# Attention and a gMLP block on one core: x of the second batch turned by DMA, with a new order of steps

## The chip, the cores and the metric

The kernel runs on one core of a Trainium2 chip. The metric is the time of one execution in microseconds of the device; lower is better. The kernel before took 160.62 us (median of three runs, 160.41 to 160.88).

## The reference

Two blocks follow one another, on 4 batches of 768 positions. The first is attention with 8 heads of 64, where a query sees the 128 last positions and the first 4 ("sinks"). Its output, x (768 x 512 per batch), goes through a gated block with a residual:

```python
keep = is_sink | in_window
scores = np.where(keep, scale * q @ k.T, -1e9)
x = softmax(scores) @ v                       # per head, heads side by side: 768 x 512
h = gelu_tanh(x @ w_in)                       # 768 x 1024
u, v = h[..., :512], h[..., 512:]
v_n = (v - mean(v)) / sqrt(var(v) + 1e-6) * g_ln
v_s = einsum('ts,bsd->btd', w_sg, v_n) + b_sg[None, :, None]
out = x + (u * v_s) @ w_out
```

## The kernel before

**A list of steps.** The order of all the work is written out by hand in one string, `STEPS` (lines 16 to 64), of 659 words. A loop at the end (lines 593 to 598) calls one function per word. A step's instructions join the queue of the engine they run on, each queue runs in the order of the list, and semaphores order the queues among each other. `QK.1.2.0` is the function `QK` with the numbers 1, 2 and 0. The first number is nearly always the batch. A letter at the end names the engine where there is a choice: A for ScalarE (ACT), D for VectorE (DVE), P for GpSimd (POOL); a mask without a letter runs on DVE.

**Loads.** `LQ`, `LK` and `LV` load q, k and v, `LW` the halves of w_in, `LWS` the halves of w_sg and `LWO` w_out. All but the very first are issued by GpSimd, between its other work. At most eight of GpSimd's loads are under way: the trace shows it at rest before a load until the eighth load before that one has landed. `LG` and `LC` load constants by SyncE.

**Attention.** A batch has four pairs of heads, p = 0 to 3. For batches 0 to 2, `TQ` and `TK` (lines 302 to 314) turn q and k of a pair on TensorE, 12 turns into PSUM, and `EQ` and `EK` copy the result out, on ACT or DVE. For batch 3 (`TURN`, line 72) SyncE issues a DMA that turns it (line 318) and there is no `TQ` or `TK`. `QK` makes the scores of two tiles of positions, `EX` takes the exponential on ACT, and `MK` masks, on DVE in one instruction or on POOL in two. `KS`, `SK` and `SX` do the sink scores: `KS` writes the first four keys of all pairs of a batch into a small tile (DVE, four instructions from batch 1 on), `SK` multiplies it by all q of the batch, so it follows the last of the batch's copies of k, and `SX` is its exponential. `AV` multiplies by v, half a batch's positions (three tiles of 128) per step, and `NR` divides and writes x for that pair and half.

**x turned.** The gated block needs x with its columns on the partitions, in the tile `xT`, of which there is one. For batches 0 and 1, `XT` (line 431) turns six blocks of 128 x 128 on TensorE and `XE` (line 438) copies them out of PSUM, on ACT or DVE: four of each per batch. For batches 2 and 3, `XD` (line 442) has SyncE issue one DMA that turns half a batch: three tiles of 512 columns, 12 blocks, 384 KB. It waits for the four `NR` of its half.

**The gated block.** `MV` makes two tiles of the v half of h (eight products, line 453), `GV` its GELU, `BN`, `RS` (POOL) and `NM` the statistics, `Z` the normalised tile, on ACT or DVE. `MV.b.0` needs the first half of x alone, `MV.b.1` both. `MU` and `GU` are the same for u; `MU.b.0` and `MU.b.1` need the first half of x, the others the second. For batch 0 the first `MV` and `MU` are cut in two, with `MA` and `UA`. `SP` multiplies z by w_sg, which `WT` has turned on TensorE and `WE` copied; it needs all of z. `GT` and `GM` do the gate, `OU` the last product, `RA` (DVE) adds x, and `ST` stores a tile of 128 x 512 by SyncE. For batch 3 the last three tiles (`LAST`, line 75) are done in halves, `OU` and `OB`, `RA` and `RB`, `ST` and `SB`.

**Buffers.** PSUM has a ring `mm` of four (lines 134 to 135) for `TQ`, `TK`, `AV`, `XT`, `WT`, `SK`, `SP` and `OU`, and a ring `sc` of two for `QK`, `MV` and `MU`. A step takes the next buffer and waits until its last reader is done. Output tiles `ot` have three buffers, so `RA` waits for the third store before it.

**SyncE's queue** runs the `EQ` and `EK` of batch 3, the `XD` and all stores, in the order of the list.

Of the kernel before, what the change touches and what calls it, by code (L numbers as in the profile page):

```python
# [13 lines left out]


STEPS = """
ZERO IDEN LQ.0.0 LK.0.0 LQ.0.1 FILL LK.0.1 LC VSK MASK LK.0.2 MASK0 CQ.0.0.A LK.0.3 HM.7 TQ.0.0 CK.0.0.A LV.0.0
EQ.0.0.D HM.1 TK.0.0 LQ.0.2 EK.0.0.A TQ.0.1 LQ.0.3 EQ.0.1.D QK.0.0.2 QK.0.0.1 LV.0.1 EX.0.0.2 VSM.0 TK.0.1 LV.0.2
KS.0.0 SK.0.0 TK.0.2 LV.0.3 EK.0.1.A MK.0.0.2.D QK.0.0.0 TK.0.3 EX.0.0.1 EK.0.2.D LQ.1.0 KS.0.1 EX.0.0.0 LW.0 KS.0.2
QK.0.1.1 MK.0.0.1.D SK.0.1 EX.0.1.1 MK.0.0.0 QK.0.1.2 LW.1 TQ.0.2 SX.0.1 QK.0.1.0 EQ.0.2.D MK.0.1.1.P EX.0.1.2  # L20
AV.0.0.0 AV.0.0.1 EK.0.3.A LWS.0 NR.0.0.0 QK.0.2.1 EX.0.1.0 NR.0.0.1 TQ.0.3 MK.0.1.2.P SK.0.2 EQ.0.3.D EX.0.2.1
QK.0.2.0 LQ.1.2 AV.0.1.1 KS.0.3 EX.0.2.0 MK.0.1.0 LWS.1 QK.0.3.1 SK.0.3 NR.0.1.1 EX.0.3.1 AV.0.1.0 MK.0.2.1.P QK.0.3.0
NR.0.1.0 XT.0.2 SX.0.3 QK.0.2.2 EX.0.3.0 XE.0.2.D MK.0.3.1.P XT.0.0 XE.0.0.D TQ.1.0 EX.0.2.2 LK.1.0 QK.0.3.2 MK.0.2.0
TQ.1.1 EQ.1.0.A LK.1.2 MK.0.3.0 AV.0.2.0 EX.0.3.2 LQ.2.0 AV.0.3.0 NR.0.2.0 EQ.1.1.A MK.0.2.2.P MA.0.0 NR.0.3.0 LWO
MK.0.3.2.D XT.0.1 AV.0.2.1 XE.0.1.A AV.0.3.1 NR.0.2.1 MV.0.0 LV.1.0 VSM.3 UA.0.0 GV.0.0 NR.0.3.1 MU.0.0 VSM.1 XT.0.3
VSM.2 WT.0 LG LV.1.1 XE.0.3.A WT.2 BN.0.0 WT.1 GU.0.0 MV.0.2 WE.1 LV.1.2 WE.2 MV.0.1 WE.0 GV.0.2 BN.0.2 MU.0.2 GV.0.1
TQ.1.2 BN.0.1 RS.0.2 GU.0.2 WT.4 MU.0.1 EQ.1.2.A LV.1.3 WE.4 RS.0.1 TQ.1.3 NM.0.2 GU.0.1 TK.1.0 TK.1.1 EQ.1.3.A
Z.0.4.D LV.2.0 WT.5 NM.0.1 Z.0.5.D MU.0.3 EK.1.1.A Z.0.2.D EK.1.0.A Z.0.0.D LV.2.1 TK.1.3 Z.0.3.D GU.0.3 QK.1.0.2 WE.5
TK.1.2 EK.1.3.A Z.0.1.D QK.1.0.1 EK.1.2.D WT.3 EX.1.0.2 LK.2.0 SP.0.0.3 WE.3 KS.1.0 SP.0.0.0 GT.0.0.3 EX.1.0.1
MK.1.0.2.P SP.0.1.1 GT.0.0.0 GM.0.0.3.D LQ.2.2 QK.1.1.2 GM.0.0.0.D QK.1.0.0 TQ.2.1 EX.1.1.2 GT.0.1.1 MK.1.0.1.P TQ.2.0  # L30
EQ.2.1.A SP.0.1.0 GM.0.1.1.D LV.2.2 EX.1.0.0 MK.1.1.2.D QK.1.2.2 GT.0.1.0 SK.1.0 LV.2.3 EQ.2.0.A QK.1.1.1 MK.1.0.0
SP.0.0.2 SX.1.0 GM.0.1.0.P EX.1.2.2 AV.1.0.1 LK.2.2 GT.0.0.2 EX.1.1.1 QK.1.2.1 MK.1.2.2.D AV.1.0.0 LV.3.0 EX.1.2.1
NR.1.0.1 SP.0.1.2 NR.1.0.0 MK.1.1.1.P QK.1.3.2 QK.1.2.0 GT.0.1.2 EX.1.3.2 SP.0.1.3 LV.3.1 MK.1.2.1.D EX.1.2.0
MK.1.3.2.D AV.1.1.1 LV.3.2 GT.0.1.3 AV.1.2.1 MK.1.2.0 QK.1.3.1 QK.1.3.0 LV.3.3 EX.1.3.1 TK.2.1 NR.1.1.1 AV.1.2.0
NR.1.2.1 EK.2.1.A XT.1.2 GM.0.1.2.P QK.1.1.0 NR.1.2.0 XE.1.2.A TK.2.0 MK.1.3.1.P TQ.2.3 EX.1.1.0 EK.2.0.D TQ.2.2
SP.0.0.1 GM.0.1.3.P EQ.2.3.A LQ.3.0 GM.0.0.2.D OU.0.4 EQ.2.2.A MK.1.1.0 EX.1.3.0 GT.0.0.1 OU.0.5 RA.0.4 AV.1.1.0
GM.0.0.1.P RA.0.5 QK.2.0.2 ST.0.4 QK.2.1.2 AV.1.3.1 EX.2.0.2 NR.1.1.0 ST.0.5 LK.3.0 TK.2.3 EX.2.1.2 MK.1.3.0 TK.2.2
# [596 lines left out]
```

## Time and profile before

| what | value |
|---|---|
| median of three runs | 160.62 us |
| the profiled execution, in all | 160.88 us |
| its span, first to last instruction | 159.2 us |
| granted TensorE clock | 0.995 of full speed |
| turns of x on TensorE (line 436), both batches | 48, 4.1 us busy |
| copies of turned x out of PSUM, ACT / DVE | 5 of 806 ns / 3 of 555 ns |
| copies of turned q and k, ACT / DVE | 17 of 811 ns / 7 of 954 ns |
| masks, DVE (line 382) / POOL (lines 386 and 390) | 26 of 745 ns / 22 pairs, the first of each 668 ns |
| `XD`, DMA from issue to landing, least / median / most | 3.6 / 3.7 / 5.3 us |
| stores, the same | 1.8 / 2.3 / 6.6 us |

The profile tells, of one execution on the chip, when each instruction ran and, from semaphores, what released an engine that stood idle. An engine's busy time is a sum over its instructions. Where the text speaks of a step's time, it is found by counting an engine's instructions off against the list.

The order of time: batch 0's attention until 28 us, batch 0's gated block beside batch 1's attention until about 70, batch 1's `MV` and `MU` from 69.5 to 81.8, batch 2's from 99 to 113 and batch 3's from 128 to 140. The last loads land at 84.5. Batch 0's `XT` steps run from 19.7 to 28.4, batch 1's from 56.2 to 68.4.

### The profile page before, as it was taken

To read this page: it belongs to the slowest core of one execution; us is meant where nothing else is said; L and a number is where in the kernel's file an instruction comes from. 1 tells how busy PE (TensorE), PEld (TensorE's weight loads), DVE (VectorE), ACT (ScalarE), POOL (GpSimd) and SP (SyncE) were. 2 spreads that over 40 slices of the span, in tenths; PEclk is the share of its full clock that TensorE was granted. 3 is DMA by queue.
4 is the path that set the end of the run, shared out by engine and by line. 5 is a ranking of instruction groups with operands and counts; after the bars stand their busy time and mean duration, and the time that the engine had idled before them with its cause. 6 is when DMAs were issued, how large, how long until landed. Compare 5 with 4: busy or idle time off the path is not lost.

```text
span 159.2 us, 3831 instructions
## 1 busy us (share of the span) xinstructions
PE 146.4 (92%) x1516; PEld 86.8 (55%) x1528; DVE 127.9 (80%) x302; ACT 102.9 (65%) x121; POOL 86.6 (54%) x119
## 2 busy tenths in 40 slices
PE   4947899899999899999999999999999999999980
PEld 1435566556656566545565664445656654555640
DVE  5467998979998999965997996389989946988661
ACT  3579997478988498896887658945984225580000
POOL 7998995349398999992303675004057310302620
PEclk9999999999999999999999999999999999999997
DMA  4999999999999999999999548310300590120145
GB/s 159 181 149 164 189 210 204 208 245 204 175 144 166 181 175 155 222 191 217 152 119 176 115 84 199 116 66 13 123 0 1 102 296 1 66 97 37 53 151 198
DMA packets 63442, 22.70 MB, mean 143 GB/s; under 512 B 51392, under 2 KB 60608, under 8 KB 63424
## 3 DMA queue, kind: packets, MB, share of 16 engines
q0 software_dynamic: 45488, 11.80, 83.5%
q1 hardware_dynamic: 17936, 10.66, 28.1%
q8 instruction: 12, 0.20, 0.5%
q14 instruction: 6, 0.05, 0.1%
HBM read 24.81 MB, written 6.29 MB: 195 GB/s over the span
## 4 chain that ended last, share of the span: by engine, by line
PE 69%; DMA 14%; DVE 7%; POOL 5%; issue 3%; DVEq 0%; SPq 0%
PE mm L538 19%; PE sc L505 12%; PE sc L453 12%; PE mm L554 9%; DMA wsg_gated<-in_moe_w_sg_dram 8%; PE sc L367 5%; DMA v_sb<-in_v_dram 5%; PE mm L308 3%; PE mm L407 3%; DVE ot L562 2%; PE mm L413 2%; PE mm L528 2%; PE mm L417 2%; POOL k L195 1%; DMA out_dram<-ot 1%
## 5 line engine op out<-in xcount | busy, mean ns | idle before, releaser
L375 ACT ACTIVATE P<-sc 128x1024 bf16<-128x1024 f32 (+1 forms) x48 | 43.9, 963 | 12.4 <-PE sc L367 12.3
L538 PE MATMUL mm<-wsgT,z 128*128 128x384 bf16 x192 | 34.2, 326 | 0.0
L386 POOL TENSOR_SCALAR_AFFINE_SELECT P<-P 128x512 bf16<-128x512 bf16 x22 | 14.7, 668 | 20.2 <-ACT P L375 14.6
L538 PEld LDWEIGHTS <-z 128*128 128x128 bf16 x192 | 17.8, 98 | 12.1 <-issue 1.4
L554 PE MATMUL mm<-w_out_sb,wsg_gated 128*128 128x512 bf16 (+1 forms) x102 | 23.0, 354 | 1.3 <-POOL wsg_gated L548 0.7
L543 DVE SCALAR_TENSOR_TENSOR gtmp<-mm,g_sb,b_bc 128x384 bf16<-128x384 f32 x32 | 19.5, 613 | 5.0 <-PE mm L538 4.8
L505 PE MATMUL sc<-xT,w_in_sb 128*128 128x384 bf16 x128 | 22.9, 326 | 0.0
L476 DVE BATCH_NORM_STATS2 st<-vt 128x6 f32<-128x512 f32 x24 | 16.2, 676 | 7.4 <-ACT vt L467 7.4
L453 PE MATMUL sc<-w_in_sb,xT 128*128 128x512 bf16 x92 | 21.8, 379 | 0.2
L484 POOL TENSOR_TENSOR rs<-rs,neg_half 128x2 f32<-128x2 f32 (+1 forms) x8 | 6.9, 867 | 27.1 <-DVE rs L479 26.2
L562 DVE TENSOR_TENSOR ot<-mm,x_sb 128x512 f32<-128x512 f32 (+1 forms) x27 | 16.6, 628 | 5.4 <-PE mm L554 5.1
L548 POOL TENSOR_TENSOR wsg_gated<-gtmp,uT 128x384 bf16<-128x384 bf16 x14 | 13.1, 942 | 11.4 <-DVE gtmp L543 11.3
L221 POOL DMA_DIRECT2D v_sb<-in_v_dram x16 | 16.6, 1046 | 4.9 <-DMA wsg_gated<-in_moe_w_sg_dram 1.7
L382 DVE TENSOR_TENSOR P<-P,mask 128x1024 bf16<-128x1024 bf16 (+1 forms) x26 | 19.1, 745 | 0.0
L427 DVE TENSOR_TENSOR x_sb<-mm,rcp 128x384 bf16<-128x384 f32 x32 | 17.8, 557 | 1.1
L467 ACT ACTIVATE vt<-sc 128x1024 f32<-128x1024 f32 x12 | 12.2, 1023 | 9.9 <-PE sc L453 9.9
L521 ACT ACTIVATE uT<-sc 128x768 bf16<-128x768 f32 x16 | 12.8, 806 | 7.6 <-PE sc L505 7.6
L407 PE MATMUL mm<-v_sb,P 128*128 128x65 bf16 x192 | 16.7, 194 | 0.7 <-DVE x_sb L427 0.3
L505 PEld LDWEIGHTS <-w_in_sb 128*128 128x128 bf16 x128 | 12.4, 98 | 8.8
L407 PEld LDWEIGHTS <-P 128*128 128x128 bf16 x192 | 14.3, 98 | 4.6 <-issue 1.9
L367 PE MATMUL sc<-qT,kT 64*128 64x256 bf16 x192 | 15.5, 264 | 0.8 <-ACT kT L226 0.6
L413 PE MATMUL mm<-v_sb,P 128*128 128x65 bf16 x160 | 15.5, 194 | 0.8 <-POOL P L390 0.8
(77 smaller groups left out, 224.6 us busy)
## 6 DMA issues: line engine op xcount, KB each, us to landing
out_dram<-ot SPq DMA_DIRECT2D x21, 256.0 KB, 3.3
v_sb<-in_v_dram POOLq DMA_DIRECT2D x16, 192.0 KB, 11.6
q<-in_q_dram POOLq DMA_DIRECT2D x4, 384.0 KB, 12.7
k<-in_k_dram POOLq DMA_DIRECT2D x4, 384.0 KB, 14.5
wsg_gated<-in_moe_w_sg_dram POOLq DMA_DIRECT2D x2, 576.0 KB, 14.8
w_in_sb<-in_moe_w_in_dram POOLq DMA_DIRECT2D x2, 512.0 KB, 11.8
qn<-in_q_dram POOLq DMA_DIRECT2D x4, 192.0 KB, 11.2
kn<-in_k_dram POOLq DMA_DIRECT2D x4, 192.0 KB, 9.9
```

The costliest lines, as they stand in the source:

```text
L367: nc.tensor.matmul(sc[:, hl, 256 * jl:256 * jl + n], kT[b, p][rows, 128 * j:128 * (j + 1)], qT[b, p][rows, 128 * j:128 * j + n], start=Tru ...
L375: nc.scalar.activation(out=pt[:, :, 0:w], in_=sc_ring[b, p, g][:, :, 0:w], func=AF.Exp, scale=scale)
L382: nc.vector.tensor_mul(pt[:, :, 0:w], pt[:, :, 0:w], m.unsqueeze(1).to_broadcast([128, 2, w]))
L407: nc.tensor.matmul(av[:, il, hl, :], P[b, p, i // 2][:, hl, 256 * (i % 2):256 * (i % 2) + 128], vb[:, h, i, :], start=first, stop=False)
L413: nc.tensor.matmul(av[:, il, hl, :], P[b, p, j // 2][:, hl, 256 * (j % 2) + 128:256 * (j % 2) + 256], vb[:, h, j, :], start=False, stop=False)
L427: nc.vector.tensor_mul(xs[:, 3 * half:3 * half + 3, :].rearrange("p t (h d) -> p t h d", h=H)[:, :, heads(b, p), :], av[:, :, :, 0:Dh], rc ...
L453: nc.tensor.matmul(hp[:, jl, :], xT[b][:, j, c, :], w_in_sb[:, c, d_half:2 * d_half], start=(c == 0), stop=(c == KD - 1))
L505: nc.tensor.matmul(hp[:, n, 0:NH], w_in_sb[:, c, 128 * dc:128 * (dc + 1)], xT[b][:, 3 * hf:3 * hf + 3, c, :], start=(c == 0), stop=(c == K ...
L538: nc.tensor.matmul(ps[:, 0:NH], z[b][:, si, 128 * dc:128 * (dc + 1)], wsgT[:, si, NH * hf:NH * (hf + 1)], start=(si == 0), stop=(si == NT ...
L543: nc.vector.scalar_tensor_tensor(out=gtmp.new((b, hf, dc)), in0=mm_ring["g", b, hf, dc][:, 0:NH], scalar=g_sb[:, dc:dc + 1], in1=b_bc[:, N ...
L554: nc.tensor.matmul(mm_ring["o", b, t][:, cols], gatedT[:, (2 * b + hf) % 3, dc, 128 * tl:128 * (tl + 1)], w_out_sb[:, dc, cols], start=(dc ...
L562: nc.vector.tensor_add(ot.get((b, t))[:, cols], mm_ring["o", b, t][:, cols], x_sb[b][:, t, cols])
```

## The change

Only the list differs: 653 words after, in a new order from end to end. Every function is as it was.

- **x of batch 1.** `XT.1.0` to `XT.1.3` (24 turns) and their copies `XE.1.0.D`, `XE.1.1.A`, `XE.1.2.A` and `XE.1.3.A` are gone; `XD.1.0` and `XD.1.1` are new. x of batch 0 is still turned on TensorE.
- **Engines.** Copies of turned q and k: 17 on ACT and 7 on DVE before, 13 and 11 after. Copies of batch 0's x: 2 on ACT and 2 on DVE before, 1 and 3 after. `CK` moves from ACT to DVE. Masks: 26 on DVE and 22 on POOL before, 29 and 19 after. `GM`: 18 on DVE and 14 on POOL before, 16 and 16 after. `Z`: 8 on ACT and 16 on DVE before, 9 and 15 after.
- **Order of GpSimd's loads.** Before: LQ.0.1, LK.0.1 to 0.3, LV.0.0, LQ.0.2, LQ.0.3, LV.0.1 to 0.3, LQ.1.0, LW.0, LW.1, LWS.0, LQ.1.2, LWS.1, LK.1.0, LK.1.2, LQ.2.0, LWO, LV.1.0. After: LQ.0.1, LK.0.1 to 0.3, LQ.0.2, LQ.0.3, LV.0.0, LQ.1.0, LV.0.1 to 0.3, LW.0, LW.1, LWS.0, LWS.1, LK.1.0, LK.1.2, LQ.1.2, LQ.2.0, LWO, LV.1.0. For batch 3 LK.3.2 comes last in place of LQ.3.2.
- **SyncE's queue** between batch 0's stores and batch 2's x. Before: ST.0.4, 0.5, 0.3, 0.0, 0.2, EQ.3.1, EQ.3.0, EK.3.0, EK.3.2, ST.0.1, EK.3.3, EQ.3.2, EQ.3.3, EK.3.1, XD.2.0. After: ST.0.0, 0.1, 0.2, XD.1.0, XD.1.1, ST.0.4, 0.3, EQ.3.0 to 3.3, ST.0.5, EK.3.0 to 3.3, XD.2.0.
- **The last three tiles** are done in halves in both lists, with the same steps.

The start and the middle of the list, old and then new:

```diff
-ZERO IDEN LQ.0.0 LK.0.0 LQ.0.1 FILL LK.0.1 LC VSK MASK LK.0.2 MASK0 CQ.0.0.A LK.0.3 HM.7 TQ.0.0 CK.0.0.A LV.0.0
-EQ.0.0.D HM.1 TK.0.0 LQ.0.2 EK.0.0.A TQ.0.1 LQ.0.3 EQ.0.1.D QK.0.0.2 QK.0.0.1 LV.0.1 EX.0.0.2 VSM.0 TK.0.1 LV.0.2
-KS.0.0 SK.0.0 TK.0.2 LV.0.3 EK.0.1.A MK.0.0.2.D QK.0.0.0 TK.0.3 EX.0.0.1 EK.0.2.D LQ.1.0 KS.0.1 EX.0.0.0 LW.0 KS.0.2
-QK.0.1.1 MK.0.0.1.D SK.0.1 EX.0.1.1 MK.0.0.0 QK.0.1.2 LW.1 TQ.0.2 SX.0.1 QK.0.1.0 EQ.0.2.D MK.0.1.1.P EX.0.1.2
-AV.0.0.0 AV.0.0.1 EK.0.3.A LWS.0 NR.0.0.0 QK.0.2.1 EX.0.1.0 NR.0.0.1 TQ.0.3 MK.0.1.2.P SK.0.2 EQ.0.3.D EX.0.2.1
-QK.0.2.0 LQ.1.2 AV.0.1.1 KS.0.3 EX.0.2.0 MK.0.1.0 LWS.1 QK.0.3.1 SK.0.3 NR.0.1.1 EX.0.3.1 AV.0.1.0 MK.0.2.1.P QK.0.3.0
-NR.0.1.0 XT.0.2 SX.0.3 QK.0.2.2 EX.0.3.0 XE.0.2.D MK.0.3.1.P XT.0.0 XE.0.0.D TQ.1.0 EX.0.2.2 LK.1.0 QK.0.3.2 MK.0.2.0
-TQ.1.1 EQ.1.0.A LK.1.2 MK.0.3.0 AV.0.2.0 EX.0.3.2 LQ.2.0 AV.0.3.0 NR.0.2.0 EQ.1.1.A MK.0.2.2.P MA.0.0 NR.0.3.0 LWO
-MK.0.3.2.D XT.0.1 AV.0.2.1 XE.0.1.A AV.0.3.1 NR.0.2.1 MV.0.0 LV.1.0 VSM.3 UA.0.0 GV.0.0 NR.0.3.1 MU.0.0 VSM.1 XT.0.3
...
-MK.1.0.2.P SP.0.1.1 GT.0.0.0 GM.0.0.3.D LQ.2.2 QK.1.1.2 GM.0.0.0.D QK.1.0.0 TQ.2.1 EX.1.1.2 GT.0.1.1 MK.1.0.1.P TQ.2.0
-EQ.2.1.A SP.0.1.0 GM.0.1.1.D LV.2.2 EX.1.0.0 MK.1.1.2.D QK.1.2.2 GT.0.1.0 SK.1.0 LV.2.3 EQ.2.0.A QK.1.1.1 MK.1.0.0
...
-NR.1.0.1 SP.0.1.2 NR.1.0.0 MK.1.1.1.P QK.1.3.2 QK.1.2.0 GT.0.1.2 EX.1.3.2 SP.0.1.3 LV.3.1 MK.1.2.1.D EX.1.2.0
-MK.1.3.2.D AV.1.1.1 LV.3.2 GT.0.1.3 AV.1.2.1 MK.1.2.0 QK.1.3.1 QK.1.3.0 LV.3.3 EX.1.3.1 TK.2.1 NR.1.1.1 AV.1.2.0
-NR.1.2.1 EK.2.1.A XT.1.2 GM.0.1.2.P QK.1.1.0 NR.1.2.0 XE.1.2.A TK.2.0 MK.1.3.1.P TQ.2.3 EX.1.1.0 EK.2.0.D TQ.2.2
-SP.0.0.1 GM.0.1.3.P EQ.2.3.A LQ.3.0 GM.0.0.2.D OU.0.4 EQ.2.2.A MK.1.1.0 EX.1.3.0 GT.0.0.1 OU.0.5 RA.0.4 AV.1.1.0
-GM.0.0.1.P RA.0.5 QK.2.0.2 ST.0.4 QK.2.1.2 AV.1.3.1 EX.2.0.2 NR.1.1.0 ST.0.5 LK.3.0 TK.2.3 EX.2.1.2 MK.1.3.0 TK.2.2
-QK.2.0.0 NR.1.3.1 EK.2.3.A QK.2.0.1 XT.1.0 MK.2.1.2.D EK.2.2.A AV.1.3.0 XE.1.0.D MK.2.0.2.P OU.0.3 EX.2.0.1 NR.1.3.0
-OU.0.0 EX.2.0.0 KS.2.0 XT.1.3 RA.0.3 MK.2.0.1.P QK.2.1.1 XE.1.3.A QK.2.1.0 RA.0.0 ST.0.3 SK.2.0 LK.3.2 EX.2.1.1
-MK.2.0.0 XT.1.1 ST.0.0 OU.0.2 EX.2.1.0 MV.1.2 RA.0.2 XE.1.1.A LQ.3.2 MK.2.1.0 ST.0.2 SX.2.0 MV.1.0 GV.1.2 MK.2.1.1.P
-AV.2.0.1 AV.2.1.0 GV.1.0 BN.1.2 MV.1.1 EQ.3.1 MU.1.1 BN.1.0 RS.1.2 GV.1.1 OU.0.1 GU.1.1 EQ.3.0 NM.1.2 BN.1.1 MU.1.3
-Z.1.4.A Z.1.5.A MU.1.2 RA.0.1 GU.1.3 RS.1.1 EK.3.0 NR.2.1.0 MU.1.0 GU.1.2 NM.1.1 NR.2.0.1 Z.1.3.A Z.1.2.D AV.2.1.1
-Z.1.1.D GU.1.0 QK.2.2.0 Z.1.0.D AV.2.0.0 EK.3.2 EX.2.2.0 NR.2.1.1 QK.2.3.1 SP.1.0.3 NR.2.0.0 SP.1.1.0 GT.1.0.3 ST.0.1
-EK.3.3 EX.2.3.1 MK.2.2.0 SP.1.0.0 GT.1.1.0 MK.2.3.1.P QK.2.3.0 GT.1.0.0 QK.2.2.1 EQ.3.2 SP.1.0.2 EX.2.3.0 GM.1.1.0.D
-GM.1.0.0.D GM.1.0.3.D EX.2.2.1 SP.1.1.1 MK.2.3.0 GT.1.0.2 EQ.3.3 MK.2.2.1.P QK.2.2.2 QK.2.3.2 GT.1.1.1 AV.2.3.0
-EX.2.2.2 SP.1.0.1 GM.1.0.2.D EX.2.3.2 GM.1.1.1.D NR.2.3.0 MK.2.2.2.P AV.2.2.0 EK.3.1 QK.3.0.0 GT.1.0.1 QK.3.0.2
...
+ZERO IDEN LQ.0.0 LK.0.0 LQ.0.1 FILL LK.0.1 LC MASK VSK LK.0.2 MASK0 CQ.0.0.A LK.0.3 HM.7 TQ.0.0 CK.0.0.D LQ.0.2
+EQ.0.0.D TK.0.0 LQ.0.3 EK.0.0.A TQ.0.1 LV.0.0 QK.0.0.0 KS.0.0 EQ.0.1.D QK.0.0.2 SK.0.0 EX.0.0.0 LQ.1.0 VSM.0 TK.0.1
+LV.0.1 EK.0.1.D HM.1 TK.0.2 LV.0.2 EX.0.0.2 MK.0.0.0 QK.0.0.1 TK.0.3 LV.0.3 EK.0.2.A KS.0.1 MK.0.0.2.D QK.0.1.2 SK.0.1
+EX.0.0.1 EK.0.3.D LW.0 SX.0.1 KS.0.2 QK.0.1.0 KS.0.3 LW.1 EX.0.1.2 MK.0.0.1.D TQ.0.2 TQ.0.3 EX.0.1.0 MK.0.1.2.P
+QK.0.1.1 EQ.0.3.D AV.0.0.0 EQ.0.2.A AV.0.0.1 LWS.0 MK.0.1.0 QK.0.3.0 EX.0.1.1 SK.0.2 NR.0.0.0 LWS.1 SK.0.3 EX.0.3.0
+QK.0.2.1 MK.0.1.1.D TQ.1.0 LK.1.0 NR.0.0.1 SX.0.3 TQ.1.1 QK.0.2.2 EX.0.2.1 MK.0.3.0 LK.1.2 AV.0.1.1 EQ.1.0.D EQ.1.1.A
+AV.0.1.0 MK.0.2.1.P QK.0.3.1 EX.0.2.2 NR.0.1.0 LQ.1.2 EX.0.3.1 NR.0.1.1 QK.0.2.0 XT.0.0 MK.0.2.2.P XT.0.2 EX.0.2.0
+XE.0.0.D QK.0.3.2 LQ.2.0 MK.0.3.1.D AV.0.2.1 EX.0.3.2 MK.0.2.0 AV.0.3.0 XE.0.2.A MK.0.3.2.P NR.0.2.1 AV.0.2.0 MA.0.0
+NR.0.3.0 LWO AV.0.3.1 NR.0.2.0 NR.0.3.1 XT.0.1 XE.0.1.D UA.0.0 LV.1.0 VSM.1 MV.0.0 VSM.3 MU.0.0 GV.0.0 XT.0.3 VSM.2 LG
+LV.1.1 WT.1 XE.0.3.D WT.2 WT.0 WE.1 GU.0.0 MV.0.1 BN.0.0 WE.0 MU.0.2 LV.1.2 GV.0.1 WE.2 WT.3 BN.0.1 GU.0.2 MV.0.2 WE.3
...
+MK.1.0.1.P QK.1.1.2 GT.0.0.3 QK.1.1.0 EX.1.1.2 SP.0.1.3 GM.0.1.0.P EX.1.1.0 AV.1.0.1 GM.0.0.3.P GT.0.1.3 QK.1.1.1
+NR.1.0.1 QK.1.3.0 LK.2.0 SP.0.0.2 EX.1.1.1 MK.1.1.2.D LK.2.2 MK.1.1.0 EX.1.3.0 SP.0.0.1 LV.3.0 MK.1.1.1.D QK.1.3.2
+GT.0.0.2 QK.1.0.0 LV.3.1 AV.1.1.0 EX.1.3.2 GT.0.0.1 AV.1.1.1 EX.1.0.0 NR.1.1.0 GM.0.0.1.P QK.1.2.1 SP.0.1.1 NR.1.1.1
+EX.1.2.1 LQ.3.0 MK.1.0.0 QK.1.3.1 QK.1.2.0 GM.0.0.2.D AV.1.0.0 MK.1.3.0 OU.0.0 EX.1.3.1 NR.1.0.0 GM.0.1.3.P OU.0.1
+RA.0.0 EX.1.2.0 MK.1.2.1.P GT.0.1.1 QK.1.2.2 ST.0.0 EX.1.2.2 RA.0.1 TQ.2.3 LQ.3.2 OU.0.2 MK.1.2.0 ST.0.1 EQ.2.3.A
+MK.1.3.1.D AV.1.2.0 TK.2.0 RA.0.2 MK.1.2.2.P AV.1.3.0 NR.1.2.0 EK.2.0.A ST.0.2 TK.2.1 NR.1.3.0 MK.1.3.2.P TQ.2.2
+EK.2.1.A QK.2.0.2 EQ.2.2.D QK.2.0.1 XD.1.0 EX.2.0.2 AV.1.2.1 LV.3.2 GM.0.1.1.D AV.1.3.1 EX.2.0.1 NR.1.2.1 MK.2.0.2.P
+QK.2.1.1 OU.0.5 NR.1.3.1 EX.2.1.1 MK.2.0.1.P TK.2.3 RA.0.5 QK.2.1.0 MK.2.1.1.P TK.2.2 EK.2.3.D EX.2.1.0 OU.0.3 LV.3.3
+EK.2.2.D QK.2.1.2 QK.2.0.0 XD.1.1 RA.0.3 EX.2.1.2 OU.0.4 LK.3.0 KS.2.0 EX.2.0.0 MK.2.1.2.D SK.2.0 MK.2.1.0 MV.1.0
+SX.2.0 MK.2.0.0 RA.0.4 AV.2.1.1 LK.3.2 GV.1.0 AV.2.0.1 NR.2.1.1 AV.2.1.0 ST.0.4 ST.0.3 EQ.3.0 AV.2.0.0 NR.2.0.1 MU.1.1
+NR.2.1.0 NR.2.0.0 MV.1.1 GU.1.1 BN.1.0 EQ.3.1 MV.1.2 GV.1.1 BN.1.1 MU.1.2 GV.1.2 EQ.3.2 MU.1.3 BN.1.2 RS.1.1 GU.1.2
+MU.1.0 GU.1.3 NM.1.1 RS.1.2 Z.1.0.A EQ.3.3 Z.1.2.D QK.2.2.1 Z.1.1.A NM.1.2 Z.1.3.D GU.1.0 Z.1.4.D Z.1.5.D EX.2.2.1
+QK.2.2.0 SP.1.1.1 ST.0.5 SP.1.1.3 GT.1.1.1 EX.2.2.0 MK.2.2.1.D SP.1.0.2 GM.1.1.1.P GT.1.1.3 EK.3.0 QK.2.3.0 GT.1.0.2
+QK.2.2.2 SP.1.1.0 EX.2.3.0 GM.1.1.3.D GM.1.0.2.D MK.2.2.0 EX.2.2.2 SP.1.0.1 EK.3.1 GT.1.1.0 MK.2.2.2.P QK.2.3.1
+GT.1.0.1 QK.2.3.2 SP.1.1.2 EX.2.3.1 GM.1.1.0.D MK.2.3.0 EK.3.2 EX.2.3.2 AV.2.2.1 MK.2.3.1.P GT.1.1.2 QK.3.0.0 NR.2.2.1
+QK.3.0.2 AV.2.2.0 EX.3.0.0 MK.2.3.2.P AV.2.3.0 NR.2.2.0 EK.3.3 SP.1.0.3 EX.3.0.2 GM.1.1.2.P NR.2.3.0 QK.3.1.0
+MK.3.0.2.P GT.1.0.3 QK.3.1.2 OU.1.3 EX.3.1.0 XD.2.0 GM.1.0.3.D EX.3.1.2 OU.1.4 MK.3.0.0 RA.1.3 QK.3.0.1 MK.3.1.2.P
+QK.3.1.1 RA.1.4 EX.3.0.1 AV.2.3.1 KS.3.0 SP.1.0.0 EX.3.1.1 MK.3.0.1.P NR.2.3.1 SK.3.0 ST.1.4 ST.1.3 OU.1.5 XD.2.1
+MK.3.1.1.D SX.3.0 GM.1.0.1.D AV.3.1.1 MK.3.1.0 MV.2.0 GT.1.0.0 RA.1.5 GM.1.0.0.D OU.1.1 GV.2.0 ST.1.5 OU.1.0 RA.1.1
+OU.1.2 ST.1.1 RA.1.0 MV.2.2 BN.2.0 ST.1.0 RA.1.2 MV.2.1 GV.2.2 ST.1.2 NR.3.1.1 BN.2.2 MU.2.3 GV.2.1 AV.3.0.0 BN.2.1
...
```

## The prediction

> **What bounds the kernel now.** I read the busy shares first, then the busy time by stretch, then the timelines of TensorE, VectorE and SyncE counted off against the step list, and last the DMA answers for single stretches.
>
> ```profile
> PE 146.4 (92%) x1516; PEld 86.8 (55%) x1528; DVE 127.9 (80%) x302; ACT 102.9 (65%) x121; POOL 86.6 (54%) x119
> PEclk9999999999999999999999999999999999999997
> DMA  4999999999999999999999548310300590120145
> ```
>
> TensorE is busy 146.4 of 159.2 us at full clock, and the DMA engines until slice 22 (some 87 us). The average hides where VectorE is as full as TensorE:
>
> ```profile
> 28.77:39.80 11.03, 10.97 (x121) 6.85 (x124) 9.79 (x25) 7.54 (x10) 6.93 (x7) 1.00 1.29 220
> 39.80:69.50 29.70, 28.32 (x400) 17.85 (x403) 28.04 (x58) 25.16 (x32) 26.44 (x33) 1.00 2.42 173
> 69.50:81.80 12.30, 12.25 (x91) 6.91 (x91) 9.38 (x26) 9.95 (x13) 4.48 (x6) 1.00 1.82 179
> ```
>
> After the stretch and its length stand PE, PEld, DVE, ACT, POOL. From 28.77 (first turn of w_sg) to 69.5 (first product of batch 1's x with w_in) PE is busy 39.3 of 40.7 and DVE 37.8. Ahead of that, the start is tied to loads:
>
> ```profile
> 15.55 13.18 DMA wsg_gated<-in_moe_w_sg_dram
> 28.77 1.18 PE mm L528 x18
> ```
>
> This is the chain of waits: TensorE reaches WT at 28.77 as LWS.0 lands.
>
> **The change, part by part.** Times are of the profiled execution (span 159.2, in all 160.88; the runs' median is 160.62, so I take 0.26 off at the end). A step's price on PE is its distance to the next step's start in the PE timeline: turn of q or k 0.46, QK 0.31, AV 0.38 (half 0) or 0.63 (half 1), OU 0.86, SK 0.33, MV 1.73, MU 1.30, SP 0.97.
>
> *The turns that go.* Four XT steps, 24 turns. Six take 0.34 in a row in the chain, and 0.44 to 0.46 to the next start elsewhere: 4 x 0.40 = **1.6 us** less on PE (1.4 to 1.8). Added up over the new order, 0.7 of it lies between WT and batch 1's first MV, 0.9 behind (SP is nowhere changed in number). Three ACT copies of 0.81 and one DVE copy of 0.56 go too; ACT has room, so they count nothing by themselves. Steps traded between ACT, DVE and POOL are counted next.
>
> *The halves of the last three tiles.* LAST is (3, 4, 5) in both kernels and their steps stand in both lists: nothing.
>
> *The start.* The first 13 GpSimd loads are the same set in another order, and LWS.0 is the 14th in both, so I leave WT at 28.77. The same PE steps stand ahead of it (18.5 us by the prices). DVE has about 3 us more there (CK, one more copy out of PSUM, two more masks) and was busy only 5.7 and 7.7 of the first two tens: 0, and up to 1.2 if that cover fails.
>
> *DVE, from WT to MV.1.0.* Copies of turned q and k on DVE go from 2 to 5 (0.95 each, +2.9), Z from 6 to 4 (0.54, -1.1), RA from 4 to 5 (0.69), masks in wider forms +0.2: 2.7 more on an engine with 2.9 to spare. KS.2.0 gates SK.2.0, the step ahead of MV.1.0. Summed by rows, the DVE steps from 28.9 to the end of KS.2.0 are 34.7 before and 38.4 after; the 34.7 ended at 67.25 in truth, 3.7 later than without a wait, partly from masks such as this:
>
> ```profile
> 58.90 1.39 DVE L382 TENSOR_TENSOR P<-P,mask 128x1024 bf16<-128x1024 bf16 x1
> 66.03 1.22 DVE L335 TENSOR_TENSOR ks_sink<-kT,halfsel 128x8 bf16<-128x8 bf16 x4
> 69.52 3.40 PE L453 MATMUL sc<-w_in_sb,xT 128*128 128x512 bf16 x15
> ```
>
> So KS.2.0 ends between 67.3 and 71.0; I take 69.8, since much of that is instructions that ran longer than their like while POOL was nearly full, and POOL stays so (26.4 of 29.7, no less work in the new order). MV.1.0 could then start at 70.1, where PE alone would come at 69.5 - 0.7 = 68.8: **+1.3** (0 to +2.5). On the way the mm ring has four buffers, so turns and AV steps wait for NR and the copies.
>
> *XD.1.0 and XD.1.1.* Each moves half of x: 12 blocks of 128x128, 384 KB. SyncE issues one in 1.44 us. What a transpose costs depends on what else moves:
>
> ```profile
> xT<-x_sb SPq DMA_TRANSPOSE x4, 3.7
> ...
> qT<-qn SPq DMA_TRANSPOSE x4, 9.7
> ```
> ```profile
> out_dram<-ot SPq DMA_DIRECT2D x2, 256.0 KB, 6.5
> ```
> ```profile
> q1 hardware_dynamic: 2168, 0.58, 95.8%
> q0 software_dynamic: 1865, 0.24, 66.3%
> ```
>
> The first are the median microseconds from issue to landing: 3.7 for the halves of batches 2 and 3, which ran after the loads were done, and 9.7 for half as many bytes of q while loads still came. The second answer is for 61 to 63 us: a store issued there took 6.5 (the shortest of all takes 1.8). The third is for 76 to 82, transposes beside loads: 2168 packets of 256 B in 6 us, 361 per us; a half is 1536 packets. XD.1.0 falls into this loaded stretch, as batch 3's loads still come. It waits for NR.1.3.0. Its DVE sum is 31.9 after 28.9, with a share of the waits as above 63.1. Ahead of it on SyncE's queue are ST.0.0, ST.0.1 and ST.0.2; the last, by the same counting, goes out at 61.8. Low end: lands as in the quiet rows, 63.1 + 3.7 = 66.8, hidden. High end: 9.7 as for q and 2.1 more for its second half of packets at the loaded rate, 75. Taken, being nearest to the 61-to-63 row in place and company: ST.0.2 lands at 68.3, its packets end some 1.5 sooner (as at 80.7 against 82.2 for the q transposes), 66.8; 1536/361 = 4.25 more is 71.05; 0.75 to land gives 71.8. PE has 7.9 us of steps between AV.1.3.0 and MV.1.0 (TK, TQ, 2 QK, 2 AV, QK, OU, TK, QK, TK, OU, 2 QK, OU, SK), and on the DVE pace it stands at MV.1.0 at 70.1: **+1.7** (0 to +5). Queued behind MV.1.0 on PE are AV.2.1.1 to AV.2.0.0, MU.1.1 and all that follows. XD.1.1 goes out at about 66, its packets follow the first's, landing near 76.5; MV.1.1 comes 5.05 after MV.1.0 starts (MV, four AV, MU), 76.8: covered by 0.3, a cover that goes with any further store between them.
>
> In sentences of their own: the Trainium skill, page Advanced Engine Details and Errata, section X-Bar Transpose (TRN2), says that on this chip a transpose DMA is as fast as a plain one, 350 to 400 GB/s expected; the quiet rows here show about 215 GB/s in the middle of XD.2.0. By that page a half needs about an estimated 1.1 us of moving, the wait of XD.1.0 is nil and the sum would be 160.6. The page VectorE: DVE Perf Modes, section The three transpose paths, speaks against the change: 390 ns a block on TensorE, 1309 ns by DMA, TensorE advised where PSUM will do. By it, as an estimate, 12 blocks one after the other are 15.7 us and the kernel would be near 169; the 3.7 us row for 12 blocks says that the blocks overlap.
>
> *SyncE and the loads later.* EQ.3 and EK.3 come behind two XD more and fewer stores. In the old order the last was issued at 88.1 and KS.3.0 began at 95.9. I count some 3 us later for both, so nothing; if that cover went, QK.3.0.0 would pay up to 2. GpSimd's order loses an old stall: PE waited 0.85 at AV.1.1.1 for a mask on POOL behind LV.3.0; now that mask is DVE's. That is within the DVE estimate.
>
> *z of batch 1.* Between its last MV and first SP stand 3 MU and 2 QK, 4.5 us, in place of 7.6; GV 1.0, BN 1.8, RS 0.7, NM 0.15 and two Z of 0.54 take 4.7 and hand-overs: **+0.3** (0 to 0.7).
>
> Sum: -1.6 + 1.3 + 1.7 + 0.3 = +1.7: 162.6 for the profiled execution, **162.3** against the median.
>
> **The rivals.**
> 1. *The transposes are hidden and the turns are a plain gain.* For it: quiet halves land in 3.7, PE is the busiest engine. Against: loads run to 84 us. -1.6 + 0.3, DVE's part absorbed by its 2.9 of idle: 159.3. Chance 0.25.
> 2. *VectorE takes the gain, the transposes stay hidden* (landed by 70.1): -1.6 + 1.3 + 0.3 = 0, 160.6. For it the 37.8 busy of 40.7; against it the 6.5 us stores. Chance 0.17.
> 3. *Both halves are late.* One mechanism: SyncE's queue is served in order behind three stores at the loaded rate. If XD.1.0 lands at 75, MV.1.0 starts 4.9 after 70.1; XD.1.1 then follows at 80, when PE comes to MV.1.1. -1.6 + 1.3 + 4.9 + 0.3 = +4.9: 165.5. It is slower than no change from a landing at 70.1 on. Chance 0.12.
> The forecast above, a moderate wait: 0.46.
>
> **How the numbers follow.** The likeliest gives 162.3, its own range 161.2 to 163.9. A measurement of this kernel can tell about 0.3% (0.5 us) from no change. Faster by more: rival 1, 0.25, and a little of 2: 0.27. Within: most of 2 and the edge of the forecast: 0.17. Slower: 0.56. The range 159.2 to 164.8 leaves out half of rival 3 and the better part of a full 1.8 us gain, under 0.2 together.
>
> **What would show it.** Right: PE idle before the first L453 of batch 1, released by DMA xT; the two new transposes taking 6 us or more; DVE over 38.5 busy between WT and there; WT still near 28.8. Wrong: the transposes landing in under 5 us, or MV.1.0 starting before 69.5; a later WT would put the loss at the start, and PE waiting at QK.3 for kT or at SP.1 for z would put it later than I do.

## The result, and the profile after

The kernel after is slower: 1.0356 times the time before (95% interval 1.0321 to 1.0391), that is 166.3 us beside 160.5. The profiled execution took 166.28 us, its span is 163.9 (before 160.88 and 159.2). Two of the four executions took 169.0 and 170.4 us at a granted clock of 0.98; the ratio leaves them out, as all ratios below leave out their like. The prediction had the direction, 162.3 us and an upper bound of 164.8: between the two profiled executions the loss is 5.4 us where it had 1.7.

From the page of the kernel after, engines and slices as before:

```profile
PE 145.3 (89%) x1491; PEld 85.2 (52%) x1504; DVE 131.7 (80%) x307; ACT 97.7 (60%) x113; POOL 84.9 (52%) x115
PEclk9999999999999999999999999999999999999999
DMA  5999999999999999999999938731000572130324
```

PE has 1.1 us less to do and takes 4.7 longer over it, so the loss is idle time. The DMA engines are busy through 23 slices of 4.1 us, to 94 us, where before they were free at 87. The busy time by stretch, cut at the first turn of w_sg, the first QK of batch 1 (before, 0.4 us ahead of it), the first MV of batch 1 and the end of its last MU:

```profile
29.69:40.83 11.14, 11.09 (x126) 7.14 (x125) 10.12 (x27) 7.58 (x11) 6.42 (x7) 1.00 1.32 219
40.83:72.70 31.87, 27.82 (x379) 16.41 (x377) 28.69 (x60) 25.52 (x30) 28.36 (x36) 1.00 2.41 174
72.70:85.05 12.35, 12.24 (x108) 7.24 (x112) 8.40 (x25) 5.96 (x7) 1.73 (x2) 1.00 1.77 163
```

In the middle one PE (first after the comma) stands idle for 4.0 of 31.9 us; before it was 1.4 of 29.7. TensorE's own waits, over the whole span (for what, total us, times, longest):

```profile
PE sc L453 <- DMA xT<-x_sb: 2.7, 1, 2.7
...
PE sc L367 <- ACT uT L521: 1.4, 1, 1.4
PE mm L407 <- DMA v_sb<-in_v_dram: 1.2, 2, 0.7
PE mm L308 <- DVE gtmp L543: 1.1, 1, 1.1
```

Four new waits, in order of time: AV steps of batch 0 for loads of v (L407, 0.4 at 14.9 and 0.7 at 18.9 us); TQ.2.3 for a PSUM buffer that GT.0.1.1 on VectorE gives back (L308, 58 us); MV.1.0 for XD.1.0 (L453); QK.2.2.0 for a score buffer that GU.1.0 gives back (L367, 86 us). GT.0.1.1 is late for TQ.2.3 because two VectorE steps ahead of it ran long: GM.0.0.2 took 1.07 us from 55.22 and MK.1.3.0 1.12 after it, where their like take 0.36 and 0.68. GpSimd was issuing LQ.3.0 from 54.6 to 56.7. In the other traces with the new order one or both of the two run long at this place as well; that the issuing is the cause is not shown. A fifth wait is in two pieces, in AV.0.2.1, for the two instructions of a mask on POOL (start, length, engine, line):

```profile
23.14 0.20 PE L407 MATMUL mm<-v_sb,P 128*128 128x65 bf16 x1 [0.54 <-POOL P L386]
...
23.96 0.20 PE L413 MATMUL mm<-v_sb,P 128*128 128x65 bf16 x1 [0.44 <-POOL P L390]
```

The exponential was ready at 20.2; POOL first ran MK.0.2.1 and issued LQ.1.2, and came to this mask at 22.0. Around the wait for XD.1.0, TensorE's timeline and SyncE's:

```profile
69.60 0.40 PE L353 MATMUL mm<-qT,ks_sink 128*32 128x512 bf16 x4
72.70 1.90 PE L453 MATMUL sc<-w_in_sb,xT 128*128 128x512 bf16 x7 [2.70 <-DMA xT<-x_sb]
```
```profile
61.79 0.33 SPq L565 DMA_DIRECT2D out_dram<-ot  x1
63.22 8.10 SPq L444 DMA_TRANSPOSE xT<-x_sb  x2
```

SK.2.0 runs at 69.6, MV.1.0 could follow at 70.0 and follows at 72.7, when XD.1.0, issued at 63.22, has landed: some 9.4 us. The wait ahead of SP.1:

```profile
84.49 1.51 ACT L493 ACTIVATE z<-vt,nmr,rs 128x512 bf16<-128x512 f32 x2
84.98 0.39 PE L367 MATMUL sc<-qT,kT 64*128 64x256 bf16 x4
...
85.13 1.46 DVE L496 TENSOR_SCALAR z<-vt,rs,nmr 128x512 bf16<-128x512 f32 x3
85.90 0.79 ACT L521 ACTIVATE uT<-sc 128x768 bf16<-128x768 f32 x1
...
86.75 0.40 PE L367 MATMUL sc<-qT,kT 64*128 64x256 bf16 x4 [1.37 <-ACT uT L521]
...
87.08 2.12 PE L538 MATMUL mm<-wsgT,z 128*128 128x384 bf16 x12
```

The named releaser is GU.1.0, queued on ACT behind two Z. But z itself is written until 86.59, so SP.1 could not have begun more than 0.5 us ahead of its 87.08: of this wait some 0.9 is for z, with another name, and the rest is GU.1.0 and the QK that waits for it.

**How the loss adds up.** For each step I take its start less the priced work ahead of it on PE (the prediction's prices); what this lag grows by is idle time. After less before: up to WT +0.92, from there to where MV.1.0 could start +0.38, the wait for XD.1.0 +2.70, up to SP.1 +1.34, from there to SP.3 +0.31; less 1.68 of work: 3.97, and SP.3.1.2 starts 145.16 - 141.19 = 3.97 later. The last products end 4.40 later, the span is 4.7 longer, and outside the span lie 0.7 more.

### The profile page after: what moved, and what is told of

It is laid out like the page before. It is cut to its first block, busy times and chain, and to the rows that moved or that the text cites. A ratio compares the mean times of both kernels' runs of the same rounds, so it can differ in the third digit from the quotient of the medians.

```text
span 163.9 us, 3765 instructions
## 1 busy us (share of the span) xinstructions
PE 145.3 (89%) x1491; PEld 85.2 (52%) x1504; DVE 131.7 (80%) x307; ACT 97.7 (60%) x113; POOL 84.9 (52%) x115
## 4 chain that ended last, share of the span: by engine, by line
PE 65%; DMA 15%; DVE 9%; POOL 4%; issue 2%; ACT 2%; POOLq 1%; DVEq 0%
PE mm L538 19%; PE sc L453 12%; PE sc L505 12%; PE mm L554 9%; DMA v_sb<-in_v_dram 6%; DMA xT<-x_sb 6%; PE sc L367 4%; DMA q<-in_q_dram 3%; DVE x_sb L427 3%; PE mm L308 3%; PE mm L407 2%; DVE P L382 2%; PE mm L413 2%; DVE ot L562 2%; PE mm L417 1%
## 5 line engine op out<-in xcount | busy, mean ns | idle before, releaser
L484 POOL TENSOR_TENSOR rs<-rs,neg_half 128x4 f32<-128x4 f32 (+1 forms) x8 | 7.3, 912 | 36.4 <-DVE rs L479 33.7
L453 PE MATMUL sc<-w_in_sb,xT 128*128 128x512 bf16 x91 | 21.9, 379 | 3.1 <-DMA xT<-x_sb 2.7
L548 POOL TENSOR_TENSOR wsg_gated<-gtmp,uT 128x384 bf16<-128x384 bf16 x16 | 15.3, 965 | 14.9 <-DVE gtmp L543 10.7
L382 DVE TENSOR_TENSOR P<-P,mask 128x1024 bf16<-128x1024 bf16 (+1 forms) x29 | 21.2, 747 | 0.8 <-ACT P L375 0.5
L386 POOL TENSOR_SCALAR_AFFINE_SELECT P<-P 128x512 bf16<-128x512 bf16 x19 | 13.0, 683 | 10.7 <-ACT P L375 10.7
L407 PE MATMUL mm<-v_sb,P 128*128 128x65 bf16 x192 | 16.3, 194 | 1.7 <-DMA v_sb<-in_v_dram 1.2
L367 PE MATMUL sc<-qT,kT 64*128 64x256 bf16 x192 | 15.7, 264 | 1.8 <-ACT uT L521 1.4
L407 PEld LDWEIGHTS <-P 128*128 128x128 bf16 x192 | 14.5, 98 | 5.0 <-issue 1.6
```

The costliest lines, as they stand in the source:

```text
L367: nc.tensor.matmul(sc[:, hl, 256 * jl:256 * jl + n], kT[b, p][rows, 128 * j:128 * (j + 1)], qT[b, p][rows, 128 * j:128 * j + n], start=Tru ...
L382: nc.vector.tensor_mul(pt[:, :, 0:w], pt[:, :, 0:w], m.unsqueeze(1).to_broadcast([128, 2, w]))
L407: nc.tensor.matmul(av[:, il, hl, :], P[b, p, i // 2][:, hl, 256 * (i % 2):256 * (i % 2) + 128], vb[:, h, i, :], start=first, stop=False)
L453: nc.tensor.matmul(hp[:, jl, :], xT[b][:, j, c, :], w_in_sb[:, c, d_half:2 * d_half], start=(c == 0), stop=(c == KD - 1))
```

## The experiments

"New list" is the kernel after, "old list" the one before; every edit is one of `STEPS`. Ratios are to the kernel before.

### The order without the transposes, the transposes without the order

The new list with x of batch 1 turned on TensorE:

```diff
-XD.1.0
+XT.1.0 ... XE.1.0.A ... XT.1.1 ... XE.1.1.A
-XD.1.1
+XT.1.2 ... XE.1.2.A ... XT.1.3 ... XE.1.3.A
```

> The new order with x of batch 1 turned on TensorE after all (XT.1.0 to 1.3, copies all on ACT; no XD.1.0 and XD.1.1). Theory of several causes: the 2.5 us wait at MV.1.0 goes, batch 3's loads come some 7 us earlier again and give back 0.8, the 24 turns cost 1.6, 0.3 of it hidden: 166.3 - 2.5 - 0.8 + 1.3 = 164.3; the start, the gap ahead of SP.1 and the tail stay. Rival, the DMA transposes and what they push cause all of the loss: 160.6. Rival, the new order alone causes it: 167.5 or more.

Measured: 1.0252 (1.0189 to 1.0316). MV.1.0 starts at 72.64, as late as with the transposes. The wait at TQ.2.3 is longer than in the kernel after, as it is in most kernels with the new order (1.3 to 1.8 us in seven others, 0.6 in one):

```profile
PE mm L307 <- DVE gtmp L542: 1.6, 1, 1.6
```

So the new order alone loses some 2.5% (4.0 us); the several causes were the better guess, and the rival that the transposes cause it all falls. The rest of the loss, 1.0% (1.7 us), comes with the transposes, which the turns beat in this order.

The old list with the transposes:

```diff
-XT.1.0 XT.1.1 XT.1.2 XT.1.3 XE.1.0.D XE.1.1.A XE.1.2.A XE.1.3.A
 NR.1.3.1
+XD.1.1
 ...
 NR.1.3.0
+XD.1.0
```

> The old list with x of batch 1 by DMA and nothing else: XT.1 and XE.1 out, XD.1.1 behind NR.1.3.1 and XD.1.0 behind NR.1.3.0. They are issued near 64.5 and 66.2. If a half takes 9.4 us to land while loads run, as in the new list, and the second 4.7 more, they land at 73.9 and 78.6; MV.1.0, at 71.25 before, starts at 78.6 and the time is 160.5 + 7.3 = 167.8. Rival, the long landing belongs to the new list's queue: they land in 4 to 5 us, MV.1.2 and MV.1.0 hardly wait and the turns are a gain: 159.

Measured: 167.7 and 167.8 us, two executions beside 160.2 before, too few for an interval. This wait:

```profile
PE sc L454 <- DMA xT<-x_sb: 6.4, 2, 5.6
```

The same landing of 9 to 10 us as in the new list (XD.1.1 issued at 63.3, MV.1.2 at 72.9). Put into the old order as it stood, the transposes cost more than the whole change does. Some 1.6 us of it, by an estimate, is not the wait itself: behind it TensorE's granted clock was 0.52 for 3.35 us.

### What makes a half land late

```diff
-LQ.3.2 ... LV.3.2 ... LV.3.3 ... LK.3.0 ... LK.3.2
 MV.1.1
+LQ.3.2 LV.3.2 LV.3.3 LK.3.0 LK.3.2
```

> The new list with LQ.3.2, LV.3.2, LV.3.3, LK.3.0 and LK.3.2 issued behind MV.1.1 in place of 59 to 71 us. If XD.1.0 takes 9.4 us because its packets share the DMA engines with loads under way, it now lands within 6 us of its issue, by 69, and the wait of 2.7 at MV.1.0 is gone (under 0.3). Rival, it is the stores ahead of it or the issue itself (2.3 us): landing and wait stay within 1 us of 72.6 and 2.7. The whole time says little here, as batch 3's k comes later.

In TensorE's timeline the wait is gone, with the three stores still ahead of XD.1.0 (issued at 64.0, so it landed within 6.7 us):

```profile
70.39 0.40 PE L354 MATMUL mm<-qT,ks_sink 128*32 128x512 bf16 x4
70.72 1.90 PE L454 MATMUL sc<-w_in_sb,xT 128*128 128x512 bf16 x8
```

It is the loads under way, not the queue. Timed, in further executions:

> The new list with batch 3's loads behind MV.1.1, run before for one look at 163.66, now timed. If the wait for XD.1.0 was worth 2.6: 163.7. Rival, the one look was a lucky execution: 165.

Measured: 1.0276 (1.0224 to 1.0328), between the two guesses. Taking the 2.7 us away gains 0.8% (1.3 us), and the two intervals just touch. In the trace a part of it went earlier: WT starts at 30.23 there, and TQ.2.3 waits 1.6. The old list with the six last loads issued from 67 us on:

> The old list with x of batch 1 by DMA, as in the run of 167.8, and the loads LQ.3.0, LK.3.0, LK.3.2, LQ.3.2, LV.3.2, LV.3.3 issued from 67 us on in place of 53 to 71. If loads under way are what makes a half land late, XD.1.1 lands near 67 and XD.1.0 near 70.3; MV.1.2 waits not at all and MV.1.0 1.4: 160.5 - 1.7 + 1.4 = 160.2. Rival, the old order leaves too little time however empty the queues are: MV.1.0 waits over 3 us and the time is 162 or more.

Measured: 1.0221 (1.0162 to 1.028). MV.1.2 and MV.1.0 don't wait at all, and QK.3.0.0 starts at 89.75, 1.5 ahead of the kernel before; then k of batch 3 is late:

```profile
PE sc L368 <- DMA kT<-kn: 2.8, 1, 2.8
```

Behind this wait too the clock was halved. The two stretches, with the clock third from the end:

```profile
93.64:96.46 2.82, 0.00 (x1) 0.00 (x1) 0.92 (x4) 1.02 (x1) 1.23 (x2) 0.95 1.10 223
96.46:99.81 3.35, 3.35 (x12) 1.17 (x12) 0.99 (x4) 0.81 (x1) 0.00 (x0) 0.53 1.09 237
```

So the late k cost 2.8 us of waiting and, by an estimate from 3.35 us at 0.53, 1.6 more.

With AV.2.0.1 between MV.1.2 and MV.1.0 besides (159.6 was expected) it was 1.0281 (1.0234 to 1.0327), with a like wait for k (2.6): there was no wait left to fill.

### Are the transposes a gain once they run by themselves?

Three kernels with SyncE's queue in the order EQ.3.0, EQ.3.1, EK.3.0, EK.3.1, EK.3.2, ST.0.1, EK.3.3, EQ.3.2, EQ.3.3. The first also has LV.3.2 and LV.3.3 behind MK.3.1.1:

> The old list with x of batch 1 by DMA and batch 3's loads late, with two mends for the wait of 2.8 us that QK.3.1.2 then had for k: SyncE's queue takes EQ.3.0, EQ.3.1, EK.3.0, EK.3.1 first, and LV.3.2 and LV.3.3 (wanted at 118 us only) go out behind MK.3.1.1, near 99. In the run without these PE was 1.5 us ahead of the kernel before at QK.3.0.0. If the transposes cost nothing once they have the DMA engines to themselves, that is kept to the end: 159.2. Rival, the DMA engines are full until 92 whatever the order, and k comes late for SK.3.0: 161 or more.

Measured: 0.9998 (0.9975 to 1.0022), 160.0 us. With LV.3.2 and LV.3.3 left at 78 us:

> The same with the order of SyncE's queue alone; LV.3.2 and LV.3.3 stay at 78. If the order of the queue is what made k late: as the other, 159.2 to 159.6. If it is the load on the DMA engines: a wait for k of 1 us or more stays, 160.5 or more.

Measured: 1.0012 (0.9988 to 1.0037), so it was the queue's order. The control, with turns on TensorE:

> The control: the old list with the same late loads and SyncE queue, and x of batch 1 still turned on TensorE. If a gain of the runs beside it comes from the turns that go: 160.4, as before. Rival, it comes from the loads' order: 159.5.

Measured: 1.0037 (1.0009 to 1.0065). Beside this control the transposes gain 0.4% (0.6 us, the intervals overlap a little) where 1.7 us of TensorE's work go. In the traces PE's lag grows by 0.47 from WT to MV.1.2 with the turns and by 1.33 without them: half of the gain turns into waits. The largest that only the run without turns has is 0.51 ahead of QK.2.1.1, for a score buffer that an exponential on ACT gives back; a wait of 0.64 ahead of AV.1.2.0, for a mask on VectorE, is in both. One copy moved from VectorE to ACT:

> The old list with x of batch 1 by DMA, batch 3's loads late, and EK.2.0 on ACT in place of VectorE (0.95 us off VectorE, 0.81 onto ACT, which three copies of turned x have left). If VectorE's pace is what eats half of the 1.7 us of turns: 0.5 less than the same without it, 159.5, ratio 0.996. Rival, ACT or the buffers set the pace: 160.0, ratio 1.000.

Measured: 0.9987 (0.9968 to 1.0005). The wait ahead of AV.1.2.0 fell from 0.64 to 0.28, one of 0.75 came in AV.1.1.1, for a mask on GpSimd, and the 0.51 ahead of QK.2.1.1 stayed. No change that can be told from none, so VectorE's pace is not shown to be what eats the gain, and no version here beats the kernel before.

### Filling the waits of the new list

The four AV of batch 2, RA.0.4 and SX.2.0 ahead of MV.1.0:

> The new list with RA.0.4, SX.2.0 and the four AV steps of batch 2 (2.2 us of PE work) between SK.2.0 and MV.1.0. If both halves have landed by 76.2, the work fills the wait: 166.3 - 2.2 = 164.1. Rival, XD.1.1 lands after that: MV.1.1, which now follows MV.1.0 by 3.0 in place of 4.8 us, takes over the wait, and the time is 165.5 or more.

Measured: 1.0367 (1.032 to 1.0413). MV.1.0 follows the AV after 0.25, and then, in the middle of MV.1.1:

```profile
PE sc L454 <- DMA xT<-x_sb: 1.7, 1, 1.7
```

XD.1.1, issued at 66.9, lands near 79.5: the second half is late too, and the rival holds.

> The new list with AV.2.1.0 and AV.2.0.0 (0.76 us) moved from ahead of MU.1.1 to between QK.2.2.1 and QK.2.2.0, where PE stands idle for 1.45 before SP.1. If that idle time is the wait for z of batch 1 and MV.1.1 can come 0.76 earlier, 0.7 is gained: 165.5, and the idle time left there is 0.7. Rival, MV.1.1 waits for XD.1.1 instead: 166.3, the idle time moved and not gone.

Measured: 1.0416 (1.0363 to 1.0468). The gap ahead of SP.1 shrank by 0.7 as expected, but XD.1.0 took 10.0 us there, TensorE stood idle for 3.2, and then its clock was halved. Busy time by stretch, the clock third from the end:

```profile
68.80:72.39 3.59, 0.39 (x5) 0.09 (x5) 2.25 (x4) 2.47 (x3) 3.06 (x4) 0.98 1.60 161
72.39:75.74 3.35, 3.35 (x9) 1.19 (x10) 0.00 (x0) 0.00 (x0) 0.00 (x0) 0.51 1.90 154
```

MV.1.0 took 3.35 in place of 1.73. Loads late, the gap filled, and GT.0.1.1 moved up behind NR.1.1.1:

> The new list with three mends: batch 3's loads behind MV.1.1 (timed alone: ratio 1.0276), GT.0.1.1 moved up behind NR.1.1.1, so that TQ.2.3 finds its buffer free, and AV.2.1.0 and AV.2.0.0 in the gap ahead of SP.1. If the order's stalls are what is left of the loss: 1.6 less at TQ.2.3 and 0.7 less in the gap, ratio 1.0276 - 0.0143 = 1.013, 162.3. Rival, VectorE is full there and GT ahead only makes something else late: 1.022 or more.

Measured: 1.0294 (1.0253 to 1.0334), the rival. TQ.2.3 no longer waits; OU.0.0 does, for GM.0.0.2 on VectorE, which took 2.60 us there (0.36 is the median of its like). The gap shrank by 0.7, and QK.3 then waits for k:

```profile
PE mm L555 <- DVE wsg_gated L549: 1.8, 1, 1.8
```
```profile
PE sc L368 <- DMA kT<-kn: 1.2, 1, 1.2
```

### The start

> The old list up to GV.0.0 (130 words), the new one behind it; both beginnings hold the same steps. If the new start costs 0.9 us that is carried to the end: 165.4, WT back at 28.8 and the first MV of batch 1 0.9 earlier than 72.7. Rival, the delay is swallowed by the later wait for the transposes: 166.3, MV.1.0 still at 72.7.

> The new list up to GV.0.0, the old one behind it (x of batch 1 on TensorE). If the new start costs 0.9 us by itself: 161.5. Rival, it costs nothing where the rest is the old order: 160.6, within 0.4.

Measured: 1.0379 (1.0335 to 1.0423) and 1.0338 (1.0292 to 1.0385). Neither is clean: the two halves load in different orders, and WT waits 1.1 and 1.5 for w_sg in the one, TQ.1.2 3.0 for q in the other. Neither theory is decided by them. Next LQ.1.0 alone was moved, together with the old tail:

```diff
-LQ.1.0 VSM.0 TK.0.1 LV.0.1 ... LV.0.3
+VSM.0 TK.0.1 LV.0.1 ... LV.0.3 LQ.1.0
```

> The new list with LQ.1.0 behind LV.0.3 and with the old list's last 61 steps. If the later v loads cost 0.9 at the start and the order of the last gates 1.1 at the end, but the start's gain is partly taken by the wait for XD.1.0 (issued after NR.1.3.0, which comes earlier too): 166.3 - 0.7 - 0.8 = 164.8, no idle time over 0.8 ahead of OB.3.3. Rival, both are noise of one execution: 166.

Measured: 1.0624 (1.0587 to 1.0661):

```profile
PE mm L309 <- DMA q<-in_q_dram: 4.7, 1, 4.7
```

The new list turns q of batch 1 as early as 17 us, so it needs LQ.1.0 early; v of batch 0 pays for it. Behind this wait the clock was 0.50 for 3.35 us. The old tail is no gain either: SP.3.1.2 takes 2.7 us there in place of 1.0. All mends together:

> The new list with every mend: the loads of batch 3 behind MV.1.1, AV.2.1.0 and AV.2.0.0 in the gap ahead of SP.1, LQ.1.0 behind LV.0.3, the old last 61 steps. From 163.7 for the loads alone: 0.7 less for the gap, 0.7 for the start, 0.8 for the tail: 161.5, still 1 more than before, from the stall at TQ.2.3 (1.1) and what is left of the gap. Rival, the gains hide behind one another: 163.

Measured: 1.0527 (1.0487 to 1.0566), by the same wait for q (3.7). Over all executions profiled, WT started at a mean of 28.7 in the eight kernels with the old start and the old list behind it (28.3 to 29.4), and of 29.5 in the nine with the new start as it is (28.7 to 30.2).

## Why the prediction was right or wrong

- **The turns that go (-1.6).** 1.68 less work, right; their worth is less. With all else equal the pair above shows 0.6, where no transpose is late: the rest turns into waits. Rival 2 has VectorE take the gain; the largest new wait there was for ACT, and a copy less on VectorE changed nothing.
- **The start (0, up to 1.2).** Wrong, +0.92. "The same set in another order" looked at LWS.0 alone. LQ.1.0 went ahead of LV.0.1 to LV.0.3, and AV.0.1.1 waits 0.7 for v; LQ.1.2 now stands between MK.0.2.1 and MK.0.2.2 on POOL, and AV.0.2.1 waits 1.0 for the second mask. These two are read from the trace; no run shows either by itself. Over all kernels the new start costs 0.8 in the mean. The cover I named, VectorE's, held.
- **VectorE up to MV.1.0 (+1.3).** Right in sum by luck, and not by its parts. KS.2.0 ended at 69.42 (69.8 forecast) and MV.1.0 could start at 70.0 (70.1). But 0.92 of it came from the start, which I had at nothing, and only 0.38 from this stretch: the ring of four that I passed over in half a sentence gave 1.1 at TQ.2.3, while the old 0.85 at AV.1.1.1 went.
- **XD.1.0 (+1.7).** The mechanism was right: issue at 63.22 (63.1), landing near 72.7 (71.8) because of the loads, as the runs with late loads show. The size is 2.70, outside the 1.7 by the row chosen. The row I chose, a store's 6.5, was a little short; the 9.7 of q's transposes in the high end was nearest. In the run that waits for XD.1.1 it lands 12.6 after its issue, where I had 10.5; "covered by 0.3" held only because MV.1.0 was itself late and MV.1.1 begins with a tile of the first half.
- **z of batch 1 (+0.3, 0 to 0.7).** Wrong, 1.34. I counted two Z; on VectorE three run behind NM.1.2 (1.46 us), after BN.1.1 and BN.1.2 back to back, and GU.1.0 behind two Z on ACT held a QK ahead of SP.1 for the last 0.5. The old list had AV steps in that gap and the new one has two QK.
- **SyncE and the loads later (0).** Right: from SP.1 to SK.3.0 PE's lag does not grow (it is 0.14 less at the end), though the last load lands 7.7 later. The cover was thin: with the loads later still, QK.3 waits 1.2 to 2.8 for k.
- **Left out.** 0.31 on the way to SP.3, 0.43 in the last gates, 0.3 behind PE's end and 0.7 outside the span in this execution.

The step that failed is the sum's reading of the new order: its terms were looked for where the diff shows a new engine or DMA (VectorE's copies, the transposes), and much of the loss lies where it only shows other places in the list. Without the turns' -1.6 and XD.1.0's +1.7 the sum has +1.6 for the order alone; with x of batch 1 still turned on TensorE it measured 4.0 us. For the transposes in place of the turns the sum has +0.1; the measured rest is 1.7 us. By terms, the mis-sized ones are z of batch 1 (+0.3, measured 1.34) and XD.1.0 (+1.7, measured 2.70), and 1.74 us at the places left out had no term at all; the start's 0 and VectorE's +1.3, measured 0.92 and 0.38, cancel.

Rival 3's 165.5 came nearest in number. It was not its mechanism: XD.1.0 landed at 72.7 and not at 75, MV.1.1 did not wait for XD.1.1, and with the three stores still ahead in the queue the wait went when the loads did.

What stays open is whether an order exists that keeps the 1.7 us: each mend tried moved a wait to the next buffer, copy or load.

## What to carry to other kernels

A transpose DMA is priced by what else moves in its own stretch: the nearest row of the same kind under the same load, not the median (here 9.4 us and more beside loads, 3.7 without). Before moving a transpose off a busy engine, clear its stretch of loads that nobody waits for yet, and look what the queue then delays. In a hand-made order, reckon every ring and every in-order queue anew; here an idle gap that one filler closed mostly opened again at the next wait.

## What the hardware showed unasked

The issue itself got slower on SyncE. For the six transposes of x, least, median and most in ns, in the new list and in the old one with late loads:

```profile
L444 SPq DMA_TRANSPOSE xT<-x_sb x6: 1325/1462/5495, 63.2 to 129.9; - x6
```
```profile
L445 SPq DMA_TRANSPOSE xT<-x_sb x6: 1323/1459/1638, 64.1 to 125.0; - x6
```

XD.1.1's 5.5 us kept the queue from everything behind it; with the loads late the two transposes of batch 1 take 1.54 and 1.64 to issue.

An idle stretch of TensorE can cost twice. After 3.20 us without work its granted clock was 0.51 for 3.35 us (above), and after 5.58 in the old list with transposes 0.52 for as long. The length of the gap alone does not decide it: 2.82 us (above) and 2.62 (with AV.2.0.1 between the two MV) were followed by 0.53 and 0.52 for 3.35 us, while after 2.70 (kernel after) and 3.01 (new start) the clock stayed at 1.00. The Trainium skill, page TensorE: Matmul & The Clock Gate, section Part 1: The HAM clock gate, says that the clock falls to half after an idle window of about 3.4 us and comes back after as long a busy one. The runs here agree on the half and on the length of the slow stretch, but gaps from 2.62 us on were enough.
